# Four small edits to a two-block kernel: z's product in fp32r, a second swapped attention turn, one copy moved, and three wide products in the last pair

## The chip, the cores and the metric

The kernel runs on one core of a Trainium2 chip. The metric is device microseconds (us) of one execution. The engines are named as in the profile: PE (TensorE matmul), PEld (its weight load), DVE (VectorE), ACT (ScalarE), POOL (GpSimd) and SP (SyncE, which issues transfers). Line numbers such as L502 are those of the kernel before; in rows of the changed kernel the numbers are up to 14 higher.

## The reference

Two pre-LayerNorm blocks follow each other, on 2048 tokens of 512 channels, in fp32.

```python
h  = x + A(layernorm(x))        # linear attention, 32 heads of 16
h2 = h + B(layernorm(h))        # layernorm again, then an MLP over the tokens

# A
q, k, v = split(x @ wqkv)
phi = lambda a: concat(softmax(a @ w_phi), softmax(-(a @ w_phi)))   # per head
kv  = einsum("bhsf,bhsd->bhfd", phi(k), v)
z   = einsum("bhsf->bhf", phi(k))             # sum over all tokens
o   = (phi(q) @ kv) / ((phi(q) @ z) + 1e-6)
out = o @ wo

# B
u = gelu(einsum("bsd,sf->bdf", h, w1) + b1)   # 2048 -> 1792
y = einsum("bdf,fs->bds", u, w2) + b2         # 1792 -> 2048
```

## The kernel before

**Products.** An fp32 product is made of three fp32r products (fp32r: one pass of TensorE over fewer bits). `split` writes the high part of an operand by an ACT copy and the low part by a subtraction on DVE or POOL; `mm3` issues high·high (L69), high·low (L70) and low·high (L71). A few products are left in plain fp32, z's sum (L502) among them.

**Stages.** There are 16 tiles of 128 tokens (`NT`). First come the projections to q, k and v with the softmax exponentials, ordered by the scheduler and from the second last tile on written out by hand. Then z is made: the running sum `zacc` of the k exponentials gets its last tile by two DVE additions (L494) and is summed over the partitions by a product with a tile of ones (L502), which ACT copies to `zB` (L503). POOL multiplies `zB` into each tile's q exponentials (`s_ez`, L458).

**The attention loop** has 20 turns (`it`), and a turn works on several tiles at once. What a turn emits, engine by engine, is the order written in the loop: `s_pq` (POOL, L474), `s_ez` (POOL, L458), `s_den` (five DVE steps, ending in w), `s_tr` (PE transposes L548, copied by ACT to pht, L550), `s_num` (PE L567 reads pht; ACT copies the result to oh, L573), `s_ol` (DVE, L578), `s_wo` (PE, mm3 with oh and ol), `s_h` (residual, DVE L595), `s_moments` (ACT, L604 to L606, last of them ve), `s_rstd` (POOL, r, L611), `s_hn` (ACT L614, L624 and the high part L64, then POOL's subtraction L65 for the low part; both parts are called hs). `fills(it)` issues the first MLP product's work for an earlier tile, and reads hs: L69 needs only the high part, L70 the low one. In even turns `s_hn` stands ahead of `s_moments` and `s_tr`, in odd ones behind. Only at `it == TURN`, 6, does `s_ez` stand behind `s_hn`. At `it == TURN + 1` the additions for row sums of a tile (`q_sums`) are run once ahead of the rest.

**Sums for the MLP.** Later parts of the first MLP product are made by seven products of 2x2 blocks in place of eight, which need sums of blocks. `T_AT` is a table by turn and place in the turn that says when such sums (`t_sums`), their high parts (`t_hi`, "h0" to "h3", ACT L644, tile ht) and low parts (`t_lo`, "l0" to "l3", DVE L647) are issued.

**The second MLP product** has 8 pairs of token tiles, each of 7 steps (p) with seven block products. In `PROD` six products are wide: one 512-column matmul on the joined high and low part (L1111, whi) and one of 256 columns (L1111, wlo), each with a PSUM bank of its own; one is narrow, three matmuls of 256 columns (L1115). The last pair uses `LAST` with all seven narrow, two to a bank, four banks in all, and its results are put together on DVE (L1202 to L1219). Eight banks rotate.

**Ordering.** The attention loop and the second product have a manual order. Between the two, in the last columns of the first product (steps p = 6), PE is free to be ordered by the scheduler together with the first products of w2, and so are ACT and DVE.

Of the kernel before, what the change touches and what calls it, by code (L numbers as in the profile page):

```python
# [25 lines left out]
NG = 8  # L26
# [14 lines left out]
def block_kernel(ctx: ExitStack, tc: tile.TileContext, x, xT, wT, phic, wo, w1, b1, w2, b2,  # L41
                 kvmask, ident_in, out):
    nc = tc.nc
# [5 lines left out]
    ones = cst.tile([P, P], F32, name="ones")  # L49
# [4 lines left out]
    eps2 = cst.tile([P, 2], F32, name="eps2")  # L54
# [54 lines left out]
    X, XH, EQ, PK, VS, SQ, PS, W = {}, {}, {}, {}, {}, {}, {}, {}  # L109
# [68 lines left out]
    def turns(*lists):  # L178

        return [ops[i] for i in range(max(map(len, lists))) for ops in lists if i < len(ops)]  # L180

    def run(*lists):
        for op in turns(*lists):
            op()
# [5 lines left out]
        return e.rearrange("p g (a d) -> p (g a) d", d=DH)  # L190

    def k_ops(t, o):
        PK[t] = kk.tile([P, NG, P], F32, name="pk", bufs=len(V_NOT) + 5)
        run(logit_ops(o, PK[t], False))

    def k_logits(t):
# [10 lines left out]
    def k_norm(t, z=True):  # L207
        sk = wk.tile([P, 2 * H], F32, name="sk", bufs=2)
        nc.vector.reduce_sum(sk, heads(PK[t]), axis=AX.X)
        nc.vector.reciprocal(sk, sk)  # L210
        nc.gpsimd.tensor_mul(heads(PK[t]), heads(PK[t]), sk.unsqueeze(2).to_broadcast([P, 2 * H, DH]))  # L211
        if z and t == 0:
            nc.gpsimd.tensor_copy(zacc, PK[t])
        elif z:
            nc.gpsimd.tensor_add(zacc, zacc, PK[t])  # L215
# [158 lines left out]
    q = {"mm": 0, "logits": 0, "exp": 0, "sum": 0}  # L374
# [57 lines left out]

    ms = ExitStack()
    ms.enter_context(tc.manual_schedule(engines={ET.PE, ET.DVE, ET.Activation, ET.Pool}))
    k_norm(NT - 2, False)
    k_logits(NT - 1)
    ak1.close()
# [52 lines left out]
        wo_hi(j)  # L490
    v_kv()
    run(q_logits(0))
    for g in range(2):
        nc.vector.tensor_add(zacc[:, 4 * g:4 * g + 4, :], zacc[:, 4 * g:4 * g + 4, :], PK[NT - 1][:, 4 * g:4 * g + 4, :])  # L494
    for j in range(KD):
        wo_lo(j)
    negate()
    q_mm()
    zB = big.tile([P, NG, P], F32, name="zB", tag="big")
    for g in range(2):  # L500
        pz = ps_k.tile([P, 4, P], F32, name="pk_ps")
        nc.tensor.matmul(pz, ones, zacc[:, 4 * g:4 * g + 4, :], start=True, stop=True)  # L502
        nc.scalar.activation(zB[:, 4 * g:4 * g + 4, :], pz, AF.Identity, bias=eps2[:, 1:])  # L503
    q_exp(0)
    s_ez(0)
    s_ez(1)
# [27 lines left out]
    a2 = ExitStack()  # L534
# [164 lines left out]
    def fills(it):  # L699
        if FN[1] < it - LAG:  # L700
            fill(1, ps_q)
        if FN[0] <= it - LAG:
            fill(0, ps_f)

    T_AT = {(13, 2): "a0 b0", (14, 1): "c0 d0", (14, 2): "a2 b2", (14, 3): "h0", (15, 0): "h1", (15, 2): "c2 d2 l0", (15, 3): "h2",
            (16, 1): "l1", (16, 3): "l2", (17, 2): "a4 b4", (17, 3): "c4 d4 h3", (18, 2): "l3"}

    def t_at(it, place):
        for op in T_AT.get((it, place), "").split():
            i = int(op[1])  # L710
# [5 lines left out]
    for it in range(NT + 4):  # L716
        even = it % 2 == 0
        t_at(it, 0)
        if 0 <= it + 1 < NT:
            s_pq(it + 1)  # L720
        if it == 0:
            s_tr(0)
            s_kv()
        if it == 1:
            run(q_logits(0))
            q_mm()
            s_tr(1)
        if it > 1 and even and it <= NT:
            s_num(it // 2 - 1)
        t_at(it, 1)  # L730
        den = s_den(it + 2) if it + 2 < NT else []
        if it > 1 and even and it <= NT:
            ol = s_ol(it // 2 - 1)
            run(ol[:1] + den[:1] + ol[1:])
            den = den[1:]
        if it < NT:
            s_x(it)
        if it + 3 < NT and it != TURN:
            s_ez(it + 3)
        negate()  # L740
        q_mm()
        fills(it)
        q_exp(0)
        logits = q_logits(1)
        if it >= 4 and even:
            s_hn(it - 4)
        if it == TURN:
            s_ez(it + 3)
        if 3 <= it < NT + 3 and even:
            s_moments(it - 3)  # L750
        if it > 1 and even and it - 2 < NT:
            s_wo(it - 2)
        if 1 < it < NT:
            s_tr(it)
        if it > 1 and not even and it - 2 < NT:
            s_wo(it - 2)
        if it >= 4 and not even:
            s_hn(it - 4)
        if 3 <= it < NT + 3 and not even:
            s_moments(it - 3)  # L760
        if 3 <= it < NT + 3:
            s_rstd(it - 3)
        if it == TURN + 1:
            run(q_sums(0))
            flush()
        run(logits + (q_sums(0) if it > 0 else []), den)
        if it > 0:
            negate()
        if not logits:
            flush()  # L770
        t_at(it, 2)
        if 0 <= it - 2 < NT:
            s_h(it - 2)
        flush()
        t_at(it, 3)
# [149 lines left out]
    LAST = ((2, 1, 0, 0), (5, 5, 0, 1), (0, 0, 1, 0), (1, 4, 1, 1), (3, 6, 2, 0), (6, 2, 2, 1), (4, 3, 3, 0))  # L925
# [164 lines left out]
    for p in range(NEAR, NP):  # L1090
# [45 lines left out]
    for n, (sp, p) in enumerate(STEPS):  # L1136
        t = 2 * sp
        last = t + 2 == NT
# [4 lines left out]
                sums_w2()  # L1143
        if p == 0:
            bank = []
            for _ in range(4 if last else 7):
                pool = (ps_f, ps_q, ps_b, ps_b)[n_bank % 8 // 2]
                bank.append(pool.tile([P, 2, HD], F32, name="py", tag="pu"))
                n_bank += 1
        order = LAST if last else PROD  # L1150
        run_on = 3 if last else 2
        if p == 0:
            products(sp, [p], order[:-1] if n == 0 else order)
# [49 lines left out]
        hb = [uo.tile([P, 2, HD], F32, name=f"hb{i}", bufs=1) for i in range(2)]  # L1203
# [1 line left out]
            nc.sync.dma_start(flat(hb[i]), out[(t + i) * P:(t + i + 1) * P, :])  # L1205
            nc.vector.tensor_scalar(hb[i], hb[i], b2s[:, t + i:t + i + 1], None, op0=ALU.add)
        nc.scalar.activation(e[:, 1], bank[0][:, 0], AF.Copy)
        nc.vector.tensor_add(hb[1][:, 1], bank[0][:, 0], hb[1][:, 1])
        nc.vector.tensor_sub(u2, bank[0][:, 1], e[:, 1])
        nc.vector.tensor_sub(hb[1][:, 0], hb[1][:, 0], u2)  # L1210
        nc.vector.tensor_sub(u3, u2, bank[1][:, 0])
        nc.vector.tensor_add(hb[0], hb[0], u3.unsqueeze(1).to_broadcast([P, 2, HD]))
        nc.vector.tensor_add(hb[0][:, 0], bank[1][:, 1], hb[0][:, 0])
        nc.vector.tensor_sub(hb[1][:, 0], hb[1][:, 0], bank[1][:, 1])
        nc.vector.tensor_add(hb[0][:, 1], bank[2][:, 0], hb[0][:, 1])
        nc.sync.dma_start(out[t * P:(t + 1) * P, :], flat(hb[0]))
        for k, o, q in ((0, bank[2][:, 1], nc.scalar), (1, bank[3][:, 0], nc.sync)):
            nc.vector.tensor_add(hb[1][:, k], o, hb[1][:, k])
            q.dma_start(out[(t + 1) * P:NT * P, k * HD:(k + 1) * HD], hb[1][:, k])  # L1219

# [48 lines left out]
```

## Time and profile before

| | before |
|---|---|
| times | 516.42, 516.67, 516.90; median 516.67 us |
| profiled execution | 516.75 us, span 515.0 us |
| PE | 509.3 us busy, 99% of the span |
| DVE | 445.6 us, 87% |
| ACT | 297.7 us, 58% |
| POOL | 244.8 us, 48%, nearly all of it before 230 us |
| granted PE clock | full in all 40 slices of the span |

A row of the timeline reads: start in us, busy us, engine, line, operation, output <- input, sizes, how many instructions of the kind ran in succession, and in brackets the idle time ahead and who ended it. Starts count from the beginning of the span, which is about 1.75 us shorter than the execution's time.

### The profile page before, as it was taken

How to read it: one execution, taken by the hardware profiler on the slowest of the kernel's cores; microseconds unless marked ns; L12 is line 12 of the kernel's file. 1: busy time of each engine (PE TensorE's matmuls, PEld its weight loads, DVE VectorE, ACT ScalarE, POOL GpSimd, SP SyncE). 2: the span in 40 equal slices, each digit the busy share in tenths (PEclk: the TensorE clock that was granted, in tenths of full speed). 3: DMA queues.
4: the chain of work that ended last, by engine and by line, in shares of the span. 5: the costliest groups of instructions: out<-in, count | busy, mean ns of one | idle time of the engine just before them, and what ended most of it. 6: DMA issues, size and time to landing. Idle time of an engine off the chain costs nothing.

```text
span 515.0 us, 9359 instructions
## 1 busy us (share of the span) xinstructions
PE 509.3 (99%) x3546; PEld 438.9 (85%) x3546; DVE 445.6 (87%) x765; ACT 297.7 (58%) x494; POOL 244.8 (48%) x188
## 2 busy tenths in 40 slices
PE   8999999999999999999999999999999999999997
PEld 7888888887877777877788899998888898899897
DVE  6893999986689998877796998989989898998985
ACT  6998943424255886668976643457753444444430
POOL 2479799984999999975343300000002212211220
PEclk9999999999999999999999999999999999999999
DMA  8833311000041342334322233374136688668743
GB/s 309 278 125 120 85 48 32 1 1 2 11 156 41 103 140 86 124 124 122 113 92 83 82 105 103 102 245 140 45 123 127 159 185 166 138 148 191 165 52 74
DMA packets 36300, 58.56 MB, mean 114 GB/s; under 512 B 3744, under 2 KB 19360, under 8 KB 36256
## 3 DMA queue, kind: packets, MB, share of 16 engines
q1 hardware_dynamic: 31648, 50.85, 31.2%
q0 software_dynamic: 4032, 6.42, 9.3%
q8 instruction: 28, 0.46, 0.4%
q10 hardware_dynamic: 576, 0.69, 0.4%
q14 instruction: 16, 0.13, 0.1%
HBM read 46.81 MB, written 11.14 MB: 113 GB/s over the span
## 4 chain that ended last, share of the span: by engine, by line
PE 82%; POOL 11%; DVE 2%; ACT 2%; issue 1%; DMA 1%; SPq 0%; POOLq 0%
PE py L1111 20%; PE pu L941 12%; PE py L1115 7%; PE pu L69 7%; PE pu L70 6%; PE pu L71 6%; POOL ez L458 5%; POOL eq L474 3%; PE pv L70 3%; PE pk_ps L69 3%; PE pk_ps L70 2%; PE pk_ps L71 2%; PE pv L71 2%; PE pv L69 2%; POOL eq L176 2%; PE po L71 2%
## 5 line engine op out<-in xcount | busy, mean ns | idle before, releaser
L1187 POOL DMA_DIRECT2D out<-ot x7 | 6.2, 887 | 157.3 <-DMA wraw<-in_w 104.1
L997 ACT ACTIVATE whi<-wraw 128x1792 fp32r<-128x1792 f32 x28 | 47.7, 1703 | 44.2 <-DVE wraw L864 26.6
L1007 DVE TENSOR_TENSOR wlo<-wraw,whi 128x1792 fp32r<-128x1792 f32 x28 | 56.6, 2021 | 4.8 <-PE py L1115 4.6
L1111 PE MATMUL py<-uf,whi 128*128 128x512 f32 x210 | 57.6, 393 | 0.0
L70 PE MATMUL pu<-hs,whi 128*128 128x512 f32 x128 | 50.4, 394 | 0.2 <-POOL hs L65 0.2
L69 PE MATMUL pu<-hs,whi 128*128 128x512 f32 x128 | 50.1, 399 | 0.0
L71 PE MATMUL pu<-hs,wlo 128*128 128x512 f32 x128 | 47.9, 390 | 0.0
L458 POOL TENSOR_TENSOR ez<-eq,zB 128x1024 f32<-128x1024 f32 x16 | 38.8, 2428 | 4.5 <-ACT zB L503 4.5
L902 ACT ACTIVATE whi<-wraw 128x896 fp32r<-128x896 f32 x24 | 22.9, 955 | 31.1 <-PE pu L941 26.2
L1111 PEld LDWEIGHTS py<-uf,whi 128*128 128x128 f32 x210 | 35.8, 189 | 4.4
L1111 PEld LDWEIGHTS py<-uf,wlo 128*128 128x128 f32 x210 | 33.1, 190 | 4.6
L941 PE MATMUL pu<-ht,whi 128*128 128x256 f32 x192 | 35.6, 283 | 0.0
L1111 PE MATMUL py<-uf,wlo 128*128 128x256 f32 x210 | 34.9, 280 | 0.0
L211 POOL TENSOR_TENSOR pk<-pk,sk 128x1024 f32<-128x1024 f32 x16 | 31.1, 1944 | 6.6 <-DVE sk L210 6.6
L65 POOL TENSOR_TENSOR hs<-hb,hs 128x512 fp32r<-128x512 f32 x16 | 21.8, 1365 | 23.5 <-ACT hs L64 23.4
L550 ACT ACTIVATE pht<-tn 128x512 f32<-128x512 f32 x32 | 17.4, 597 | 26.8 <-PE tn L548 26.7
L474 POOL TENSOR_TENSOR eq<-eq,w 128x1024 f32<-128x1024 f32 x16 | 32.3, 2022 | 0.8 <-DVE w L471 0.8
L215 POOL TENSOR_TENSOR zacc<-zacc,pk 128x1024 f32<-128x1024 f32 x13 | 31.3, 2407 | 0.6
L69 PEld LDWEIGHTS pu<-hs,whi 128*128 128x128 f32 x128 | 24.0, 188 | 7.1 <-issue 2.5
L941 PEld LDWEIGHTS pu<-ht,whi 128*128 128x128 f32 x192 | 30.0, 192 | 0.0
L70 PEld LDWEIGHTS pu<-hs,whi 128*128 128x128 f32 x128 | 24.1, 188 | 5.8 <-POOL hs L65 1.4
L187 ACT ACTIVATE pk<-pk,r 128x1024 f32<-128x1024 f32 x16 | 18.4, 1150 | 18.3 <-DVE pk L165 18.3
(208 smaller groups left out, 1608.1 us busy)
## 6 DMA issues: line engine op xcount, KB each, us to landing
wraw<-in_w SPq DMA_DIRECT2D x28, 512.0 KB, 4.2
wraw<-in_w SPq DMA_DIRECT2D x48, 256.0 KB, 2.8
xraw<-in_xT SPq DMA_DIRECT2D x16, 256.0 KB, 3.2
xh<-in_x SPq DMA_DIRECT2D x16, 256.0 KB, 2.7
h<-in_x SPq DMA_DIRECT2D x16, 256.0 KB, 2.7
out<-h SPq DMA_DIRECT2D x14, 256.0 KB, 2.4
out<-ot POOLq DMA_DIRECT2D x14, 256.0 KB, 4.7
wraw<-in_wT SPq DMA_DIRECT2D x12, 256.0 KB, 5.0
```

Source lines behind the costliest of these rows:

```text
L69: nc.tensor.matmul(o, ah, bh, start=first, stop=False)
L70: nc.tensor.matmul(o, ah, bl, start=False, stop=False)
L71: nc.tensor.matmul(o, al, bh, start=False, stop=last)
L211: nc.gpsimd.tensor_mul(heads(PK[t]), heads(PK[t]), sk.unsqueeze(2).to_broadcast([P, 2 * H, DH]))
L215: nc.gpsimd.tensor_add(zacc, zacc, PK[t])
L458: nc.gpsimd.tensor_mul(EZ[t], EQ[t], zB)
L474: nc.gpsimd.tensor_mul(heads(EQ[t]), heads(EQ[t]), W[t].rearrange("p g c h -> p (g c h)").unsqueeze(2).to_broadcast([P, 2 * H, DH]))
L941: nc.tensor.matmul(ACC[p][bk][:, half], WS[p, i][x][:, a], hb[b][y], start=i == 0 and half == 0 and k == 0, stop=i == NT // 2 - 1 and k == ...
L997: nc.scalar.activation(WH[g], RAW[g], AF.Copy)
L1007: nc.vector.tensor_sub(wl_, RAW[g], WH[g])
L1111: nc.tensor.matmul(o, w, u, start=p == 0 and not low, stop=p == NP - 1, skip_group_check=True)
L1115: nc.tensor.matmul(bank[bk][:, half], AW[sp, p][x][:, a], UB[p, b][:, y], start=p == 0 and half == 0 and i == 0, stop=p == NP - 1 and i == ...
```

## The change

Four edits, independent of each other.

1. **z's product.** The sum `zacc` is split in a high part `zh` (ACT) and a low part `zl` (DVE), each half for itself, and the two fp32 products with ones become four fp32r ones, with a copy `ones_r` of the ones.
2. **The turn.** `TURN` becomes (6, 7). At it = 7 `s_hn(3)` now stands ahead of `s_moments` and `s_tr`, and `s_ez(10)` behind it. The additions of `q_sums`, of which turn 7 issued two sets, are issued once there.
3. **The table.** "h2", the high part of the third sum, moves from the end of turn 15 to the second place of turn 16.
4. **The last pair.** `ENDS` takes the place of `LAST` for the second product: products (2,1), (5,5) and (0,0) are wide, each with its own bank, so there are six banks, and three more DVE additions join the halves.

```diff
-TURN = 6
+TURN = (6, 7)
...
+    nc.scalar.activation(ones_r, ones, AF.Copy)
...
-    for g in range(2):
-        nc.vector.tensor_add(zacc[:, 4 * g:4 * g + 4, :], zacc[:, 4 * g:4 * g + 4, :], PK[NT - 1][:, 4 * g:4 * g + 4, :])
+    zh, zl = (kk.tile([P, NG, P], F32R, name=name, tag="pk", bufs=len(V_NOT) + 5) for name in ("zh", "zl"))
+    halves = [slice(4 * g, 4 * g + 4) for g in range(2)]
+    for a in halves:
+        nc.vector.tensor_add(zacc[:, a], zacc[:, a], PK[NT - 1][:, a])
+        nc.scalar.activation(zh[:, a], zacc[:, a], AF.Copy)
+    for a in halves:
+        nc.vector.tensor_sub(zl[:, a], zacc[:, a], zh[:, a])
...
-        nc.tensor.matmul(pz, ones, zacc[:, 4 * g:4 * g + 4, :], start=True, stop=True)
-        nc.scalar.activation(zB[:, 4 * g:4 * g + 4, :], pz, AF.Identity, bias=eps2[:, 1:])
+        nc.tensor.matmul(pz, ones_r, zh[:, a], start=True, stop=False)
+        nc.tensor.matmul(pz, ones_r, zl[:, a], start=False, stop=True)
+        nc.scalar.activation(zB[:, a], pz, AF.Identity, bias=eps2[:, 1:])
...
-    T_AT = {(13, 2): "a0 b0", (14, 1): "c0 d0", (14, 2): "a2 b2", (14, 3): "h0", (15, 0): "h1", (15, 2): "c2 d2 l0", (15, 3): "h2",
-            (16, 1): "l1", (16, 3): "l2", (17, 2): "a4 b4", (17, 3): "c4 d4 h3", (18, 2): "l3"}
+    T_AT = {(13, 2): "a0 b0", (14, 1): "c0 d0", (14, 2): "a2 b2", (14, 3): "h0", (15, 0): "h1", (15, 2): "c2 d2 l0",
+            (16, 1): "l1 h2", (16, 3): "l2", (17, 2): "a4 b4", (17, 3): "c4 d4 h3", (18, 2): "l3"}
...
-        if it + 3 < NT and it != TURN:
+        if it + 3 < NT and it not in TURN:
             s_ez(it + 3)
...
-        if it >= 4 and even:
+        if it >= 4 and (even or it in TURN):
             s_hn(it - 4)
-        if it == TURN:
+        if it in TURN:
             s_ez(it + 3)
...
-        if it >= 4 and not even:
+        if it >= 4 and not even and it not in TURN:
             s_hn(it - 4)
...
-        if it == TURN + 1:
-            run(q_sums(0))
+        adds = q_sums(0) if it > 0 else []
+        if it == TURN[1]:
+            run(adds)
             flush()
-        run(logits + (q_sums(0) if it > 0 else []), den)
+            adds = []
+        run(logits + adds, den)
...
+    ENDS = ((2, 1, 0, None), (5, 5, 1, None), (0, 0, 2, None), (1, 4, 3, 0), (3, 6, 3, 1), (6, 2, 4, 0), (4, 3, 5, 0))
...
-            for _ in range(4 if last else 7):
+            for _ in range(6 if last else 7):
...
-        order = LAST if last else PROD
+        order = ENDS if last else PROD
...
-        nc.vector.tensor_add(hb[1][:, 1], bank[0][:, 0], hb[1][:, 1])
-        nc.vector.tensor_sub(u2, bank[0][:, 1], e[:, 1])
+        nc.vector.tensor_add(e[:, 1], bank[0][:, 1], e[:, 1])
+        nc.vector.tensor_add(hb[1][:, 1], e[:, 1], hb[1][:, 1])
+        nc.vector.tensor_sub(u2, bank[1][:, 0], e[:, 1])
+        nc.vector.tensor_add(u2, bank[1][:, 1], u2)
         nc.vector.tensor_sub(hb[1][:, 0], hb[1][:, 0], u2)
-        nc.vector.tensor_sub(u3, u2, bank[1][:, 0])
+        nc.vector.tensor_sub(u3, u2, bank[2][:, 0])
+        nc.vector.tensor_sub(u3, u3, bank[2][:, 1])
```

POOL at turn 7, before: hs is the low part that `s_hn` makes, ez and eq belong to `s_ez` and `s_pq`, r to `s_rstd`.

```order
L611 TENSOR_TENSOR r_68<-ve_2185,mhalf 128x1
L474 TENSOR_TENSOR eq<-eq,w 128x1024
L458 TENSOR_TENSOR ez<-eq,zB 128x1024
L65 TENSOR_TENSOR hs<-hb,hs 128x512
L611 TENSOR_TENSOR r_68<-ve_2281,mhalf 128x1
```

The same place after the change:

```order
L619 TENSOR_TENSOR r_68<-ve_2195,mhalf 128x1
L476 TENSOR_TENSOR eq<-eq,w 128x1024
L65 TENSOR_TENSOR hs<-hb,hs 128x512
L460 TENSOR_TENSOR ez<-eq,zB 128x1024
L619 TENSOR_TENSOR r_68<-ve_2291,mhalf 128x1
```

hs has moved ahead of ez, one instruction earlier.

ACT in the same turn, before: L606 is the last step of `s_moments`, L550 the copies of the transposes (pht), L671 a weight's high part, L614, L624 and L64 the three steps of `s_hn(3)`.

```order
L606 ACTIVATE ve_2185<-ve_2185,eps_67 128x1
L550 ACTIVATE pht<-tn 128x4x128 x2
L671 ACTIVATE whi<-wraw 128x512 x2
L187 ACTIVATE eq<-eq,r_66 128x1024
L550 ACTIVATE pht<-tn 128x4x128 x2
L614 ACTIVATE ve_2185<-ve_2185,r_68 128x1
L624 ACTIVATE hb<-h,ve_2185,r_68 128x512
L64 ACTIVATE hs<-hb 128x512
```

After:

```order
L614 ACTIVATE ve_2195<-ve_2195,eps_67 128x1
L558 ACTIVATE pht<-tn 128x4x128 x2
L679 ACTIVATE whi<-wraw 128x512 x2
L188 ACTIVATE eq<-eq,r_66 128x1024
L622 ACTIVATE ve_2195<-ve_2195,r_68 128x1
L632 ACTIVATE hb<-h,ve_2195,r_68 128x512
L64 ACTIVATE hs<-hb 128x512
L558 ACTIVATE pht<-tn 128x4x128 x2
```

The three steps of `s_hn(3)`, which read POOL's r, have moved ahead of the second pair of pht copies.

ACT where turn 15 ends and turn 16 begins, before: ht is the copy that "h2" names, oh the copy of `s_num`.

```order
L606 ACTIVATE ve_2929<-ve_2929,eps_67 128x1
L644 ACTIVATE ht<-hb 128x1024
L671 ACTIVATE whi<-wraw 128x512
L573 ACTIVATE oh<-tn 128x512 x2
L614 ACTIVATE ve_2929<-ve_2929,r_68 128x1
```

After:

```order
L614 ACTIVATE ve_2939<-ve_2939,eps_67 128x1
L679 ACTIVATE whi<-wraw 128x512
L581 ACTIVATE oh<-tn 128x512 x2
L652 ACTIVATE ht<-hb 128x1024
L622 ACTIVATE ve_2939<-ve_2939,r_68 128x1
```

The copy ht has moved from ahead of whi and oh to behind them. On DVE z's two low parts (zl) come directly behind the two additions to zacc and ahead of wo's four low parts (wol). In the stretch between the first and the second MLP product, whose order the scheduler makes, instructions of PE, DVE and ACT are placed a few rows earlier or later; the order of SP's transfers is the same.

More of the change, by code (lines that the diff above doesn't have):

```diff
@@ L103, in block_kernel @@
     zacc = wp.tile([P, NG, P], F32, name="zacc")
+    ones_r = wp.tile([P, P], F32R, name="ones_r")
     ps_k = a1.enter_context(tc.tile_pool(name="ps_k", bufs=2, space=PSUM))
@@ L192, in k_ops @@
     def k_ops(t, o):
-        PK[t] = kk.tile([P, NG, P], F32, name="pk", bufs=len(V_NOT) + 5)
+        PK[t] = kk.tile([P, NG, P], F32, name="pk", tag="pk", bufs=len(V_NOT) + 5)
         run(logit_ops(o, PK[t], False))
@@ L499, in block_kernel @@
     zB = big.tile([P, NG, P], F32, name="zB", tag="big")
-    for g in range(2):
+    for a in halves:
         pz = ps_k.tile([P, 4, P], F32, name="pk_ps")
-        nc.tensor.matmul(pz, ones, zacc[:, 4 * g:4 * g + 4, :], start=True, stop=True)
-        nc.scalar.activation(zB[:, 4 * g:4 * g + 4, :], pz, AF.Identity, bias=eps2[:, 1:])
+        nc.tensor.matmul(pz, ones_r, zh[:, a], start=True, stop=False)
+        nc.tensor.matmul(pz, ones_r, zl[:, a], start=False, stop=True)
+        nc.scalar.activation(zB[:, a], pz, AF.Identity, bias=eps2[:, 1:])
     q_exp(0)
@@ L1207, in block_kernel @@
         nc.scalar.activation(e[:, 1], bank[0][:, 0], AF.Copy)
-        nc.vector.tensor_add(hb[1][:, 1], bank[0][:, 0], hb[1][:, 1])
-        nc.vector.tensor_sub(u2, bank[0][:, 1], e[:, 1])
+        nc.vector.tensor_add(e[:, 1], bank[0][:, 1], e[:, 1])
+        nc.vector.tensor_add(hb[1][:, 1], e[:, 1], hb[1][:, 1])
+        nc.vector.tensor_sub(u2, bank[1][:, 0], e[:, 1])
+        nc.vector.tensor_add(u2, bank[1][:, 1], u2)
         nc.vector.tensor_sub(hb[1][:, 0], hb[1][:, 0], u2)
-        nc.vector.tensor_sub(u3, u2, bank[1][:, 0])
+        nc.vector.tensor_sub(u3, u2, bank[2][:, 0])
+        nc.vector.tensor_sub(u3, u3, bank[2][:, 1])
         nc.vector.tensor_add(hb[0], hb[0], u3.unsqueeze(1).to_broadcast([P, 2, HD]))
-        nc.vector.tensor_add(hb[0][:, 0], bank[1][:, 1], hb[0][:, 0])
-        nc.vector.tensor_sub(hb[1][:, 0], hb[1][:, 0], bank[1][:, 1])
-        nc.vector.tensor_add(hb[0][:, 1], bank[2][:, 0], hb[0][:, 1])
+        nc.vector.tensor_add(hb[0][:, 0], bank[3][:, 0], hb[0][:, 0])
+        nc.vector.tensor_sub(hb[1][:, 0], hb[1][:, 0], bank[3][:, 0])
+        nc.vector.tensor_add(hb[0][:, 1], bank[3][:, 1], hb[0][:, 1])
         nc.sync.dma_start(out[t * P:(t + 1) * P, :], flat(hb[0]))
-        for k, o, q in ((0, bank[2][:, 1], nc.scalar), (1, bank[3][:, 0], nc.sync)):
+        for k, o, q in ((0, bank[4][:, 0], nc.scalar), (1, bank[5][:, 0], nc.sync)):
             nc.vector.tensor_add(hb[1][:, k], o, hb[1][:, k])
```

## The prediction

> **What bounds the kernel now.** I read the head of the page first, then the waits of TensorE, then the windows of the two stretches in which the change moves instructions, and last the timeline at each of the edited places.
>
> ```profile
> span 515.0 us, 9359 instructions
> ...
> PE 509.3 (99%) x3546; PEld 438.9 (85%) x3546; DVE 445.6 (87%) x765; ACT 297.7 (58%) x494; POOL 244.8 (48%) x188
> ```
>
> TensorE is busy 509.3 of 515.0 us. A change gains only by taking matmul time out of PE's row, or by ending one of its few waits; time on any other engine counts only where PE stands for it. Two such waits are listed that belong to edited steps:
>
> ```profile
> PE po L71 <- DVE ol L578: 0.2, 1, 0.2
> ...
> PE pu L70 <- POOL hs L65: 0.2, 1, 0.2
> ```
>
> Each is one event of 0.2 us. The timeline shows more than the list does, since a matmul that waits is partly drawn as a longer one; I measure a stall as the distance between the starts of neighbouring matmuls less their usual distance. How close the other engines follow is in the windows (columns: PE, PEld, DVE, ACT, POOL busy, then PE clock, DMA share, GB/s):
>
> ```profile
> 165.00:206.00 41.00, 40.84 (x282) 31.70 (x266) 38.87 (x68) 32.02 (x66) 40.66 (x29) 1.00 0.34 110
> ...
> 290.00:355.00 65.00, 65.00 (x525) 64.20 (x525) 59.47 (x130) 32.49 (x41) 0.00 (x0) 1.00 0.45 134
> ```
>
> In the attention loop around turns 4 to 8 (165 to 206 us) POOL is busy 40.66 of 41.00 us beside PE's 40.84: the two run in lock-step, and an earlier PE finds POOL late unless POOL moves up too. From 290 to 355 POOL is out, and DVE with 59.47 of 65 is nearest. The clock is 1.00 in all of these rows.
>
> The profiled execution took 516.75 us, 0.08 above the median of 516.67; what lies outside its span, 1.75 us, I leave as it is. A measurement of this kernel tells 0.2% (1.03 us) from no change, so "faster" begins below 515.64 and "slower" above 517.70.
>
> **Edit 1, z in fp32r.** First the rows of z and of what feeds and uses it:
>
> ```profile
> 122.45 2.15 DVE L494 TENSOR_TENSOR zacc<-zacc,pk 128x512 f32<-128x512 f32 x2
> 124.53 2.48 DVE L446 TENSOR_TENSOR wol<-wor,woh 128x512 fp32r<-128x512 f32 x4
> ...
> 125.90 1.88 PE L502 MATMUL pk_ps<-zacc,ones 128*128 128x512 f32 x4
> ...
> 127.85 0.39 PE L70 MATMUL pv<-wvl,xs 128*128 128x512 f32 x1
> ...
> 128.58 4.77 POOL L458 TENSOR_TENSOR ez<-eq,zB 128x1024 f32<-128x1024 f32 x2 [4.52 <-ACT zB L503]
> ...
> 164.59 0.55 POOL L611 TENSOR_TENSOR r<-ve,mhalf 128x1 f32<-128x1 f32 x1 [0.95 <-ACT ve L606]
> ```
>
> The usual distance of 512-column fp32r matmuls is 0.23 us: six of them start at 486.62 and the next kind at 488.00 (rows under edit 4), 1.38 / 6. From 125.90 to 127.85 is 1.95 and holds z's product and one such matmul (L69), so the product costs 1.95 − 0.23 = 1.72 for its four records. After it, four fp32r matmuls cost 4 × 0.23 = 0.92. PE saves **0.80**. The Trainium skill's page "FP8 and Floating Point Precision", section "TensorE Precision Notes", says that a true fp32 product takes four passes through the array. By it the two products would be eight passes of 0.23, 1.84, and the gain 0.92; the trace shows four records over 1.72, which is near it, and the row decides.
>
> The new operands must not be late. DVE's two adds end at 122.45 + 2.15 = 124.60. ACT's copy of the second half costs 0.63 (row at 191.15 below, the same form) and ends at 125.25, DVE's two subtractions cost 2.48 / 4 = 0.62 each and end at about 125.95. PE wants the last of them as its fourth matmul, at 125.90 + 0.69 = 126.59. That is 0.64 in hand. The four wol subtractions behind them are pushed by 1.24 to about 128.3; they are first read two turns into the loop, far behind. zB is then out 0.6 to 0.8 earlier, POOL's first ez with it: POOL had stood 4.52 us for exactly this. So POOL moves up with PE, and where it waits later (0.95 at 164.59 for ACT's ve, which itself follows PE) the releaser is early too. The 0.80 therefore goes through the lock-step stretch. Bounds: 0.3 if zl comes 0.5 late, 0.92 at most; I take 0.80.
>
> **Edit 2, the turn at it = 7.** Its rows:
>
> ```profile
> 188.05 0.99 POOL L611 TENSOR_TENSOR r<-ve,mhalf 128x1 f32<-128x1 f32 x1
> ...
> 191.00 2.38 POOL L458 TENSOR_TENSOR ez<-eq,zB 128x1024 f32<-128x1024 f32 x1
> 193.35 1.29 POOL L65 TENSOR_TENSOR hs<-hb,hs 128x512 fp32r<-128x512 f32 x1
> ...
> 199.36 1.75 POOL L65 TENSOR_TENSOR hs<-hb,hs 128x512 fp32r<-128x512 f32 x1
> ```
>
> ```profile
> 189.00 1.09 ACT L550 ACTIVATE pht<-tn 128x512 f32<-128x512 f32 x2 [0.44 <-PE tn L548]
> 189.97 0.30 ACT L614 ACTIVATE ve<-ve,r 128x1 f32<-128x1 f32 x1
> 190.30 0.82 ACT L624 ACTIVATE hb<-h,ve,r 128x512 f32<-128x512 f32 x1
> 191.15 0.63 ACT L64 ACTIVATE hs<-hb 128x512 fp32r<-128x512 f32 x1
> ```
>
> ```profile
> 191.63 1.09 PE L567 MATMUL tn<-pht,kvB 64*32 64x256 f32 x32
> ...
> 194.14 0.39 PE L69 MATMUL pu<-hs,whi 128*128 128x512 f32 x1
> 194.69 0.50 PE L70 MATMUL pu<-hs,whi 128*128 128x512 f32 x1 [0.16 <-POOL hs L65]
> 195.03 0.40 PE L71 MATMUL pu<-hs,wlo 128*128 128x512 f32 x1
> ```
>
> The low part of tile 3 (hs, POOL) came at 194.64. PE's L70 started 194.69 − 194.14 = 0.55 behind L69, 0.32 over the usual, and the next 0.34 behind that, 0.11 over: a stall of 0.43. With hs ahead of ez (2.38) on POOL it is ready two us sooner and the stall goes. Two things take most of it back. First, ACT now does tile 3's three steps before the pht copies. They wait for POOL's r, which ends at 189.04, by edit 1 at 188.24. Then 0.30 + 0.82 + 0.63 with the small gaps of the rows brings 190.0, and the two copies end at 191.1. PE's L567 reads them; it starts at 191.63 now, and at 190.83 by edit 1. It would stand about 0.3. Second, the next hs (tile 4) ended at 201.11, and PE's L70 stood 0.11 for it; since POOL is full, it moves up by edit 1's 0.80 and no more, so whatever PE won beyond that at tile 3 is waited out there. Net I take **0.1** (0.43 − 0.3, rounded down for the second). Bounds: +0.54 when neither bites (0.43 and 0.11), −0.4 when the copies come 0.5 later than I reckon. That the additions for tile 7's row sums are made once in place of twice changes nothing on PE.
>
> **Edit 3, the h2 copy.** Its rows:
>
> ```profile
> 249.21 1.05 ACT L644 ACTIVATE ht<-hb 128x1024 fp32r<-128x1024 f32 x1
> 250.16 0.61 ACT L671 ACTIVATE whi<-wraw 128x512 fp32r<-128x512 f32 x1
> 250.68 1.07 ACT L573 ACTIVATE oh<-tn 128x512 fp32r<-128x512 f32 x2
> ```
>
> ```profile
> 251.78 1.29 DVE L578 TENSOR_TENSOR ol<-tn,oh 128x512 fp32r<-128x512 f32 x2 [1.31 <-ACT oh L573]
> ```
>
> ```profile
> 251.97 0.39 PE L70 MATMUL po<-wol,oh 128*128 128x512 f32 x1
> 252.52 0.50 PE L71 MATMUL po<-woh,ol 128*128 128x512 f32 x1 [0.17 <-DVE ol L578]
> 252.86 0.39 PE L69 MATMUL po<-woh,oh 128*128 128x512 f32 x1
> ```
>
> PE stands (0.55 − 0.23) + (0.34 − 0.23) = 0.43 for ol, which DVE makes from ACT's oh; DVE itself stands 1.31 for oh. The 128x1024 copy of 1.05 us stood ahead on ACT and now comes behind, so oh is up to 0.95 earlier and ol likewise: covered twice over. The copy itself is wanted by a later subtraction (l2, a turn on). Gain **0.43**; bounds 0 (another ACT row holds oh) and 0.43.
>
> **Edit 4, the last pair.** Its rows, from the timeline, the chain that ended last, and the tail:
>
> ```profile
> 486.62 1.55 PE L1111 MATMUL py<-uf,whi 128*128 128x512 f32 x6
> 488.00 0.88 PE L1111 MATMUL py<-uf,wlo 128*128 128x256 f32 x6
> 488.71 0.40 PE L1115 MATMUL py<-uf,whi 128*128 128x256 f32 x2
> ```
>
> ```profile
> 494.13 17.64 PE py L1115 x147
> ```
>
> ```profile
> 511.79 0.42 DVE L1218 TENSOR_TENSOR hb<-py,hb 128x256 f32<-128x256 f32 x1 [0.32 <-PE py L1115]
> ```
>
> 147 narrow matmuls in 17.64 us are 0.120 each, 0.360 for the three of a product. A wide one (1.38 / 6 = 0.230) with its 256-column partner (0.71 / 6 = 0.118) is 0.348. Three products over 7 steps change, 21 × 0.012 = **0.25**. The end hangs on DVE's last adds, which wait for PE's last product (0.32) and stay as they are; the three added adds (0.42 each) belong to the banks of the first two products, which are finished earlier, so I set them at nothing. If one of them does not fit, the end is up to 0.4 later. Bounds −0.15 and 0.25.
>
> **Sum.** 0.80 + 0.10 + 0.43 + 0.25 = 1.58. From the profiled 516.75 that is 515.17; from the median, 516.67 − 1.58 = 515.09, forecast **515.1**.
>
> **The rivals.** (B) The turn gives all of its 0.54: 516.67 − 2.02 = 514.65. For it: POOL's hs at 199.36 took 1.75 where the one at 193.35 took 1.29, as a DVE subtraction had started just before it:
>
> ```profile
> 199.21 0.74 DVE L665 TENSOR_TENSOR wlo<-wraw,whi 128x512 fp32r<-128x512 f32 x1
> ```
>
> Were their order turned, POOL would have 0.46 more. On this the Trainium skill's page "SBUF — State Buffer", section "SBUF: two separate sides", has a rule: the port pair that DVE and GpSimd share is an exclusive lock, held for a whole instruction by the one that starts first. The trace agrees with it here (0.46 longer behind a start 0.15 earlier); which of them starts first after the change is open. Against it: ACT's new wait for POOL's r lies on PE's path however the port goes. Chance 0.13.
>
> (C) The turn loses instead: ACT's copies come 0.5 later than reckoned, and PE and the later tiles follow. Gain 1.58 − 0.5 = 1.08, 515.6, on the bound of 515.64. Chance 0.16, half of it on either side.
>
> (D) The lead is taken back by DVE between 290 and 355. Its lead on PE is small in places:
>
> ```profile
> 352.25 0.69 DVE L665 TENSOR_TENSOR wlo<-wlo,whi 128x512 fp32r<-128x512 f32 x1 [0.52 <-issue]
> ```
>
> ```profile
> 353.28 0.61 PE L71 MATMUL pu<-hs,wlo 128*128 128x512 f32 x2
> ```
>
> Here the low part is ready 353.28 − 352.94 = 0.34 before PE reads it. An early PE loses what exceeds this: 1.33 of lead (edits 1 to 3) less 0.34 is 1.0, so the time would be 516.67 − 0.34 − 0.25 = 516.1, no change. Against it: DVE has 5.5 us idle in those 65, so most of its work moves up with PE. Chance 0.08.
>
> (E) Slower. The stretch from 352 to 380 (the eight steps of w1's last columns, mixed with the first products of w2) is ordered by a scheduler, and the change reorders PE, ACT and DVE in it.
>
> ```profile
> 352.00:380.00 28.00, 28.00 (x134) 23.46 (x133) 26.11 (x52) 18.30 (x32) 0.00 (x0) 1.00 0.33 104
> ```
>
> PE has no gap there now, but DVE is busy 26.11 of 28. If one more DVE instruction of the 0.69 kind falls ahead of a wlo with 0.34 in hand, PE stands 0.35; over the eight steps 2.8, or 516.67 − 1.58 + 2.8 = 517.9. A late 128x1792 copy ahead of one of them would make it more. It decides the sign from a total of 1.58 on, and "slower" from 2.6. Against it: the new order puts wlo no later among its neighbours as far as the rows can be told apart. Chance 0.11.
>
> That z's product gains nothing because four matmuls take as long as two fp32 ones is excluded by the 0.23 rows: fp32r costs one record each.
>
> **The numbers.** Forecast 0.52, B 0.13, C 0.16, D 0.08, E 0.11. Faster: 0.52 + 0.13 + 0.08 = 0.73; within 0.2%: 0.08 + 0.08 = 0.16; slower 0.11. The range from 514.3 (B with an early zl and 0.92) to 516.3 (D, with 0.2 for the spread of runs) leaves out E and the ends.
>
> **What would show it.** In the profile after: z's four matmuls 0.23 apart and POOL's first ez near 127.8; at tile 3 no step between L69 and L70, but L567 waiting for ACT's pht; ol's wait near 252 gone; the last pair 0.25 shorter; no new PE wait between 345 and 385. The forecast is wrong if PE's new waits on POOL at tile 4 or on wlo after 345 sum to over 0.6, or if a zl matmul waits.

## The result and the profile after

The changed kernel takes 515.05 us (median of 8 runs, 514.78 to 515.77) against 516.61 for the kernel before (8 runs, 516.15 to 517.08): 1.56 us less, ratio 0.9971 with the interval 0.9962 to 0.998, that is 1.0 to 2.0 us (here and below the ratio is worked out over all runs, so it can differ a little from the quotient of the medians). The forecast was 515.1. The profiled execution's span went from 515.0 to 513.3.

The head of the page after, and PE's waits after (us in total, times, longest):

```profile
span 513.3 us, 9324 instructions
...
PE 508.0 (99%) x3525; PEld 437.8 (85%) x3525; DVE 447.7 (87%) x770; ACT 298.8 (58%) x497; POOL 245.2 (48%) x188
```

```profile
PE tn L575 <- ACT pht L558: 0.2, 1, 0.2
```

PE is busy 1.3 us less. The waits for ol and for hs are off the list, and a wait for ACT's pht is new. Now the edited places in the timeline after, z first:

```profile
124.31 1.33 DVE L501 TENSOR_TENSOR zl<-zacc,zh 128x512 fp32r<-128x512 f32 x2
125.55 2.49 DVE L448 TENSOR_TENSOR wol<-wor,woh 128x512 fp32r<-128x512 f32 x4
...
125.52 0.39 PE L509 MATMUL pk_ps<-zh,ones_r 128*128 128x512 f32 x1
125.75 0.39 PE L510 MATMUL pk_ps<-zl,ones_r 128*128 128x512 f32 x1
125.98 0.39 PE L509 MATMUL pk_ps<-zh,ones_r 128*128 128x512 f32 x1
126.20 0.39 PE L510 MATMUL pk_ps<-zl,ones_r 128*128 128x512 f32 x1
...
126.66 0.39 PE L70 MATMUL pv<-wvl,xs 128*128 128x512 f32 x1
...
127.52 5.14 POOL L460 TENSOR_TENSOR ez<-eq,zB 128x1024 f32<-128x1024 f32 x2 [3.83 <-ACT zB L511]
```

The four matmuls are 0.23 apart and none waits for zl. From the first of them to L70 it is 126.66 − 125.52 = 1.14 where it was 1.95: 0.81 saved. But POOL's first two ez now take 5.14 where they took 4.77: the last of the four wol is on DVE from about 127.4 to 128.04, and ez starts at 127.52. Seven us on, PE stands for it:

```profile
130.34 1.22 DVE L469 TENSOR_REDUCE tz<-ez 128x64 f32<-128x1024 f32 x1 [2.29 <-POOL ez L460]
...
133.83 0.68 DVE L162 TENSOR_TENSOR eq<-pu,mx 128x512 f32<-128x512 f32 x1
...
134.36 0.39 PE L71 MATMUL pv<-wvh,xs 128*128 128x512 f32 x1
134.65 0.47 PE L69 MATMUL pu<-wqh,xs 128*128 128x512 f32 x1
134.96 0.39 PE L70 MATMUL pu<-wql,xs 128*128 128x512 f32 x1
```

L69 opens a new product of q, whose place in PSUM DVE clears with L162 (end 134.51); it starts 0.29 behind L71 and L70 0.31 behind it, 0.14 lost together. DVE's steps before L162 start with tz, which stood 2.29 for POOL's first ez.

The turn, ACT, POOL and PE:

```profile
188.07 0.29 ACT L622 ACTIVATE ve<-ve,r 128x1 f32<-128x1 f32 x1 [0.53 <-POOL r L619]
188.39 0.82 ACT L632 ACTIVATE hb<-h,ve,r 128x512 f32<-128x512 f32 x1
189.24 0.64 ACT L64 ACTIVATE hs<-hb 128x512 fp32r<-128x512 f32 x1
189.78 1.06 ACT L558 ACTIVATE pht<-tn 128x512 f32<-128x512 f32 x2
...
189.99 1.28 POOL L65 TENSOR_TENSOR hs<-hb,hs 128x512 fp32r<-128x512 f32 x1
...
198.34 1.76 POOL L65 TENSOR_TENSOR hs<-hb,hs 128x512 fp32r<-128x512 f32 x1
...
190.90 1.10 PE L575 MATMUL tn<-pht,kvB 64*32 64x256 f32 x32 [0.21 <-ACT pht L558]
...
193.42 0.39 PE L69 MATMUL pu<-hs,whi 128*128 128x512 f32 x1
193.65 0.39 PE L70 MATMUL pu<-hs,whi 128*128 128x512 f32 x1
...
199.76 0.39 PE L69 MATMUL pu<-hs,whi 128*128 128x512 f32 x1
200.16 0.50 PE L70 MATMUL pu<-hs,whi 128*128 128x512 f32 x1
```

Tile 3's low part is there at 191.3, over two us ahead of its use, and L69 to L70 is the usual 0.23. ACT had to stand 0.53 for POOL's r first, so the pht copies end at 190.84 and PE's L575 starts 0.60 behind its predecessor (190.30) where it was 0.32: 0.28 lost. At tile 4 POOL's subtraction takes 1.76 again and L70 is 0.40 behind L69.

The h2 place, and the last pair (the chain's last row, one pair's step in the timeline, and DVE's last addition):

```profile
248.78 1.06 ACT L581 ACTIVATE oh<-tn 128x512 fp32r<-128x512 f32 x2
...
249.87 1.29 DVE L586 TENSOR_TENSOR ol<-tn,oh 128x512 fp32r<-128x512 f32 x2 [0.35 <-ACT oh L581]
...
251.02 0.39 PE L70 MATMUL po<-wol,oh 128*128 128x512 f32 x1
251.25 0.39 PE L71 MATMUL po<-woh,ol 128*128 128x512 f32 x1
```

```profile
505.81 4.33 PE py L1126 x36
```

```profile
500.01 0.86 PE L1122 MATMUL py<-uf,whi 128*128 128x512 f32 x3
500.71 0.52 PE L1122 MATMUL py<-uf,wlo 128*128 128x256 f32 x3
501.06 0.40 PE L1126 MATMUL py<-uf,whi 128*128 128x256 f32 x2
...
510.16 0.42 DVE L1232 TENSOR_TENSOR hb<-py,hb 128x256 f32<-128x256 f32 x1 [0.65 <-PE py L1126]
```

oh and ol are early enough, and PE goes from L70 to L71 at the usual 0.23. Three wide products take 501.06 − 500.01 = 1.05, 0.350 each, a narrow one 4.33 / 12 = 0.361. The last addition still waits for PE alone, so the three new ones cost nothing at the end. In the stretch that the scheduler orders, and in the one before it, PE has no gap:

```profile
290.00:355.00 65.00, 65.00 (x525) 64.22 (x524) 59.57 (x131) 33.43 (x44) 0.00 (x0) 1.00 0.46 138
352.00:380.00 28.00, 28.00 (x134) 23.43 (x133) 26.58 (x51) 19.48 (x32) 0.00 (x0) 1.00 0.32 101
```

**Where the 1.7 us of the span come from.** The start of one and the same matmul in two timelines gives PE's lead at that place. This table has it for every kernel of the study, against the profile of before (starts there in brackets; "pht" are the products L567 near those times).

| kernel | z's product (125.90) | behind z (127.85) | po of kvS (141.45) | pht (177.47) | pht (191.63) | pht (206.13) | first ht (292.00) | last (511.47) |
|---|---|---|---|---|---|---|---|---|
| changed kernel | 0.37 | 1.19 | 1.02 | 1.04 | 0.73 | 0.95 | 1.40 | 1.63 |
| z alone | 0.50 | 1.32 | 1.18 | 1.14 | 1.17 | 1.17 | 1.18 | 1.18 |
| turn alone | 0.57 | 0.56 | 0.57 | 0.55 | 0.27 | 0.54 | 0.55 | 0.55 |
| h2 alone | -0.06 | -0.06 | -0.06 | -0.06 | -0.05 | -0.07 | 0.38 | 0.38 |
| last pair alone | 0.21 | 0.21 | 0.21 | 0.21 | 0.18 | 0.15 | 0.12 | 0.35 |
| all but the turn | -0.21 | 0.61 | 0.45 | 0.44 | 0.41 | 0.39 | 0.85 | 1.07 |
| repeat of changed | -0.02 | 0.80 | 0.63 | 0.63 | 0.34 | 0.59 | 1.05 | 1.28 |
| repeat of all but the turn | 0.23 | 1.05 | 0.90 | 0.91 | 0.91 | 0.91 | 1.37 | 1.60 |
| four wol later | 0.01 | 0.83 | -4.74 | -6.51 | -6.79 | -6.51 | -6.05 | -5.82 |
| r behind eq | 0.16 | 0.98 | 0.82 | 0.75 | -0.30 | 0.29 | 0.75 | 0.97 |
| the same, no turn | -0.22 | 0.60 | 0.44 | 0.37 | -0.69 | -1.42 | -0.96 | -0.73 |
| r behind eq, one wol first | 0.33 | 1.14 | 1.15 | 1.06 | 0.03 | 0.61 | 1.07 | 1.30 |
| one wol first | 0.60 | 1.42 | 1.42 | 1.39 | 1.11 | 1.37 | 1.82 | 2.04 |

The first column is no edit's: it runs from -0.22 to 0.60, and "turn alone", whose program up to there is that of before, has 0.57. It arises in the first 9 us and then stays. There PE's 128-column matmuls start 0.21 apart at first and 0.11 apart later; the spacing changes at 4.0 us in the changed kernel (lead 0.37) and at 7.0 us in "all but the turn" (lead -0.21). The profile of before changes at 4.2 us, but then stands 0.35 for DVE's wraw, whose load came late (DVE had stood 1.07 for it). The columns behind the first are read as differences along a row. Where a row holds no edit it still drifts by up to 0.09 ("last pair alone" goes from 0.21 to 0.12 ahead of its edit), so a difference under 0.1 is not told from nothing.

### The profile page after: what moved, and what is told of

The parts are those of the page before. It is cut to its first block, busy times and chain, and to the rows that moved or that the text cites. A ratio compares the mean times of both kernels' runs of the same rounds, so it can differ in the third digit from the quotient of the medians.

```text
span 513.3 us, 9324 instructions
## 1 busy us (share of the span) xinstructions
PE 508.0 (99%) x3525; PEld 437.8 (85%) x3525; DVE 447.7 (87%) x770; ACT 298.8 (58%) x497; POOL 245.2 (48%) x188
## 4 chain that ended last, share of the span: by engine, by line
PE 86%; POOL 9%; DVE 1%; issue 1%; ACT 1%; DMA 1%; POOLq 0%
PE py L1122 21%; PE pu L951 12%; PE pu L69 7%; PE pu L70 7%; PE pu L71 7%; PE py L1126 5%; POOL ez L460 4%; PE pv L70 3%; PE pv L71 3%; PE pv L69 3%; PE pk_ps L69 3%; PE pk_ps L71 2%; PE pk_ps L70 2%; POOL eq L476 2%; PE po L71 2%; PE po L69 2%
## 5 line engine op out<-in xcount | busy, mean ns | idle before, releaser
L1122 PE MATMUL py<-uf,whi 128*128 128x512 f32 x225 | 61.9, 393 | 0.0
L70 PE MATMUL pu<-hs,whi 128*128 128x512 f32 x128 | 50.3, 393 | 0.0
L69 PE MATMUL pu<-hs,whi 128*128 128x512 f32 x128 | 50.1, 399 | 0.0
L71 PE MATMUL pu<-hs,wlo 128*128 128x512 f32 x128 | 48.0, 390 | 0.0
L1122 PEld LDWEIGHTS py<-uf,whi 128*128 128x128 f32 x225 | 38.4, 189 | 4.6
L1122 PEld LDWEIGHTS py<-uf,wlo 128*128 128x128 f32 x225 | 35.5, 190 | 5.0
L1122 PE MATMUL py<-uf,wlo 128*128 128x256 f32 x225 | 37.5, 280 | 0.0
L69 PEld LDWEIGHTS pu<-hs,whi 128*128 128x128 f32 x128 | 24.0, 188 | 7.1 <-issue 2.5
L70 PEld LDWEIGHTS pu<-hs,whi 128*128 128x128 f32 x128 | 24.1, 188 | 5.5 <-POOL hs L65 1.0
```

Source lines behind the costliest of these rows:

```text
L69: nc.tensor.matmul(o, ah, bh, start=first, stop=False)
L70: nc.tensor.matmul(o, ah, bl, start=False, stop=False)
L71: nc.tensor.matmul(o, al, bh, start=False, stop=last)
L1122: nc.tensor.matmul(o, w, u, start=p == 0 and not low, stop=p == NP - 1, skip_group_check=True)
```

## The experiments: each edit alone

The first four runs make one edit each, as in the diff above, and nothing else.

> Edit 1 alone (z's product in fp32r, the rest as before). Theory (terms of the prediction add up, the part of the lead that was there ahead of z is chance of the first loads): z's four matmuls 0.23 apart, PE 0.8 earlier behind them, about 0.15 of that lost again at the first q product behind 134 us (PE waits for a PSUM bank that DVE frees, DVE being held by POOL's ez); time 0.6 to 0.8 below before. Rival (the lead ahead of z belongs to the edit): PE is 0.35 earlier already at the start of z, time 1.1 to 1.2 below. Rival (POOL caps it): the lead is used up between 165 and 206 us, time 0 to 0.3 below.

515.96 us against 516.57, ratio 0.9988 (0.998 to 0.9997). PE's lead grows by 0.82 at z, falls by 0.14 up to the po product, and stays. That is 0.68 for the edit, the theory's number. The rival by which the 0.35 ahead of z belong to the edit falls with the first column: this run has 0.50 there, but "turn alone", without edit 1, has 0.57, and two later runs with edit 1 have -0.02 and -0.21. The cap between 165 and 206 us falls too: 1.14 at 177.47 and 1.17 at 206.13.

> Edit 2 alone (turn (6, 7)). Theory: the stall of 0.43 at tile 3's low part goes, PE stands 0.3 at the product that reads ACT's pht copies and some at tile 4's low part; net within 0.15 of nothing, time 0 to 0.15 below before, not told from it. Rival (the turn gives its full 0.54): 0.5 below. Rival (it loses): 0.3 above.

516.53 against 516.57, ratio 1.0003 (0.9994 to 1.0012). The timeline of PE has both halves of the exchange:

```profile
190.75 0.39 PE L71 MATMUL po<-woh,ol 128*128 128x512 f32 x1
191.36 1.10 PE L567 MATMUL tn<-pht,kvB 64*32 64x256 f32 x32 [0.22 <-ACT pht L550]
...
200.26 0.39 PE L69 MATMUL pu<-hs,whi 128*128 128x512 f32 x1
200.62 0.50 PE L70 MATMUL pu<-hs,whi 128*128 128x512 f32 x1
```

0.28 is lost at L567 (0.61 for 0.32), and 0.13 at tile 4 before L70 (0.36 for 0.23). In the table the lead is 0.55 before and 0.54 behind. Edit 2 gives nothing here; with edit 1 the run without the turn, below, shows the same.

> Edit 3 alone (h2 moved behind oh). Theory: PE's stall of 0.43 at the low part ol near 252 us goes and nothing takes its place; time 0.4 below before. Rival: the copy's new place delays what stands behind it on ACT (tile 12's three steps, the next pht) and PE stands there; time 0 to 0.2 below.

516.34 against 516.57, ratio 0.9992 (0.9983 to 1.0001). The lead goes from -0.07 to 0.38: 0.45, as the theory said; the time alone could not tell it from nothing.

> Edit 4 alone (three wide products in the last pair). Theory: the last pair's matmuls take 0.25 less, the tail is as long as before; time 0.25 below. Rival: the three additional additions push the last ones, the end is 0.4 later behind the last matmul, time 0.15 above.

516.38 against 516.57, ratio 0.9998 (0.9989 to 1.0007). The lead goes from 0.12 to 0.35: 0.23. The rival's 0.4 at the end did not come.

> The changed kernel without edit 2 (turn 6 alone). Theory (edit 2 moves the wait and removes none): tile 3's low part stalls PE 0.43 again, the wait for pht is gone, behind tile 4's low part PE is where it was with edit 2; time within 0.15 of the changed kernel, 1.3 to 1.6 below before. Rival (edit 2 gives 0.43 once edit 1 has moved POOL): 0.4 above the changed kernel.

515.51 us against 516.47, ratio 0.9977 (0.9968 to 0.9986). Between 177.47 and 206.13 the lead falls by 0.05, in the changed kernel by 0.09. That is the theory's nothing. The median by itself, 0.46 above the changed kernel's, would have looked like the rival; but this kernel was 0.58 behind the changed one already at the start of z, and a repeat (below) gave 514.98.

## The experiments: what holds the rest

**Four wol later.** The edit:

```diff
-    for j in range(KD):
-        wo_lo(j)
     negate()
...
     run(s_den(1))
     run(q_logits(0))
+    for j in range(KD):
+        wo_lo(j)
```

> The changed kernel with wo's four low parts on DVE moved from behind zl to behind the second tile's den and row logits. Theory (POOL's first ez is held up by DVE's wol, which the two zl push into it; DVE's q chain follows ez and frees PE's bank late): the first ez takes 2.4 in place of 2.78, PE's wait of 0.14 at the q product near 134.7 goes; what POOL has won is gone at its wait for ve at 163.6, so the time is 0.14 below the changed kernel and no more. Rival (POOL's lead lasts through the loop): 0.4 to 0.5 below, with the waits at tiles 0, 1 and 4 gone.

522.21 us against 516.47, ratio 1.0114 (1.01 to 1.0127), 5.7 slower. The timeline has the reason of the wait and of what followed it (last row: the window from 140 to 150 us, PE clock in the third column from the end):

```profile
127.88 4.76 POOL L460 TENSOR_TENSOR ez<-eq,zB 128x1024 f32<-128x1024 f32 x2 [3.84 <-ACT zB L509]
...
138.49 7.31 DVE L448 TENSOR_TENSOR wol<-wor,woh 128x512 fp32r<-128x512 f32 x4
```

```profile
146.19 0.69 PE L564 MATMUL po<-ident,kvS 128*128 128x128 f32 x2 [5.41 <-DVE kvS L530]
...
147.10 0.63 PE L70 MATMUL pu<-wql,xs 128*128 128x512 f32 x1
147.52 0.63 PE L71 MATMUL pu<-wqh,xs 128*128 128x512 f32 x1
...
140.00:150.00 10.00, 4.59 (x19) 3.64 (x17) 9.88 (x13) 2.50 (x4) 5.17 (x4) 0.66 0.66 212
```

The first half of the theory holds: the two ez take 4.76, and the lead at the q product is no longer lost there. The place for the four was wrong. In a stretch in which POOL runs one SBUF product behind the other they took 7.31 us where they take 2.49 (the first two 2.44 and 2.83, each ending 0.55 behind the end of a POOL product, eq and then ez), kvS behind them on DVE came late, and PE stood 5.41. Neither theory had this.

**r behind eq.** POOL had stood 0.94 us for ACT's ve at 163.56 in the changed kernel. The first form of this experiment put the call of `s_rstd(0)` behind the `run` of the row logits:

> The changed kernel with POOL's r of tile 0 (turn 3) moved behind the two steps of the row logits, so that POOL does these while it had stood 0.94 us for ACT's ve. Theory (POOL caps PE from 165 to 206 us): POOL is 0.9 earlier for the rest of the stretch, PE's stalls at the low parts of tiles 0, 1 and 4 (0.11, 0.25, 0.2) and at pht in turn 7 (0.28) go; time 0.6 to 0.8 below the changed kernel. Rival (PE's stalls are ACT's or DVE's, POOL is only named): 0 to 0.2 below.

> The same move of r, without edit 2. Theory: with POOL 0.9 earlier tile 3's low part comes in time without edit 2, and no pht waits for POOL; time as in the run with r moved and edit 2 kept, or up to 0.2 lower. Rival (tile 3's low part still comes late): 0.3 above that run.

Both left every engine's order as it was, since POOL's two steps are issued by `negate()`, one line further down. So these are repeats, of the changed kernel (515.21 against 516.47, ratio 0.9975, 0.9966 to 0.9984) and of it without the turn (514.98, ratio 0.9972, 0.9961 to 0.9982), and they say how far such a median moves between two series of runs. The second form moves the instruction:

```diff
-        if 3 <= it < NT + 3:
+        if 3 < it < NT + 3:
             s_rstd(it - 3)
...
         if it > 0:
             negate()
+        if it == 3:
+            s_rstd(0)
```

> The changed kernel with POOL's r of tile 0 really behind the two row-logit steps of turn 3 (in the run before it had stayed ahead of them, since these are issued by the call that follows). Theory (POOL's lateness from 165 to 206 us comes from its wait of 0.94 us for ACT's ve): POOL fills that wait, the steps behind start 0.9 earlier, PE's stalls at the low parts of tiles 0, 1 and 4 (0.11, 0.16, 0.2) and at pht in turn 7 (0.28) go, 0.7 in all; time 0.6 to 0.75 below the changed kernel. Rival (r later holds up ACT's three steps of tile 0, and POOL stands again for its next operands): 0 to 0.3 below.

515.84 us against 516.42, ratio 0.9986 (0.9977 to 0.9995), some 0.7 to 1.0 behind the changed kernel's gain. POOL does what was meant: r at 164.12 without a wait, the next eq at 164.64 in place of 165.43. The stalls that the theory names are gone too. But the gain does not come. The same DVE subtraction in the changed kernel, and then with r moved:

```profile
164.49 1.53 DVE L673 TENSOR_TENSOR wlo<-wraw,whi 128x512 fp32r<-128x512 f32 x1
```

```profile
164.12 0.55 POOL L619 TENSOR_TENSOR r<-ve,mhalf 128x1 f32<-128x1 f32 x1
164.64 1.94 POOL L476 TENSOR_TENSOR eq<-eq,w 128x1024 f32<-128x1024 f32 x1
...
164.69 2.44 DVE L673 TENSOR_TENSOR wlo<-wraw,whi 128x512 fp32r<-128x512 f32 x1
...
186.65 0.39 PE L70 MATMUL pu<-hs,whi 128*128 128x512 f32 x1
187.16 0.50 PE L71 MATMUL pu<-hs,wlo 128*128 128x512 f32 x1
```

POOL's eq now starts 0.05 ahead of DVE's wlo, which waits it out and takes 2.44. Two more of them go from 1.16 and 0.80 to 2.04 and 1.46. DVE is late, PE stands for it at 178, 181 and 187 (there 0.28 before L71, which reads wlo), and the lead falls by 1.05 between 177.47 and 191.63. Of that 0.59 comes back by 206.13, as the stalls that before has at tiles 3 and 4 are not met. From z's start to the last matmul this kernel wins 0.81, the changed one 1.26: POOL's early steps took more from DVE than they gave.

> The same without edit 2. Theory: POOL's 0.9 also covers the 0.43 at tile 3, so edit 2 is not needed: time within 0.1 of the run with edit 2, no stall over 0.1 left between 165 and 206 us. Rival: tile 3's stall stays in part, 0.2 to 0.4 above that run.

516.99 us against 516.42, ratio 1.0006 (0.9997 to 1.0015), 1.15 behind the run with the turn. Here two wlo take 4.02 us, h behind them is late, and PE stands for it:

```profile
189.14 4.02 DVE L673 TENSOR_TENSOR wlo<-wraw,whi 128x512 fp32r<-128x512 f32 x2
...
195.96 0.39 PE L71 MATMUL pu<-hs,wlo 128*128 128x512 f32 x1
197.33 0.47 PE L69 MATMUL po<-woh,oh 128*128 128x512 f32 x1 [0.98 <-DVE h L603]
```

Neither theory was right: tile 3's low part is in time, but the order of POOL's steps decides which DVE subtractions are held.

**One wol first.** Of the four, one moves into DVE's wait of 1.16 us ahead of the last row logits before z; first together with r behind eq, then alone.

```diff
     v_kv()
+    wo_lo(0)
     run(q_logits(0))
...
-    for j in range(KD):
+    for j in range(1, KD):
         wo_lo(j)
```

> r behind the row logits, and besides one of wo's four low parts moved ahead on DVE, into its wait of 1.16 us before the last row logits ahead of z. Theory (the fourth wol overlaps the start of POOL's first ez and costs it 0.37 us): the two ez take 4.77 in place of 5.14, PE's wait of 0.14 near 134.7 us goes; the lead behind it is 0.1 to 0.15 more than in the run without this move. Rival (the moved wol holds up POOL's last pk and with it zacc and zl): PE stands at zl, 0.1 to 0.5 later.

515.43 us against 516.42, ratio 0.9983 (0.9974 to 0.9992). The two ez take 4.76, and the lead behind z stays: 1.14 and 1.15, where the run without this move had 0.98 and 0.82. Behind 177 us it loses as that run does.

> The changed kernel with only the one low part of wo moved ahead on DVE, r where the changed kernel has it. Theory (what the last runs left standing): the two first ez take 4.76 in place of 5.14, PE's wait of 0.14 near 134.7 us goes and POOL follows PE behind its wait for ve, so the lead of 0.13 lasts to the end; time 0.1 to 0.15 below the changed kernel, less than the runs can tell apart, and seen only in the starts of PE's matmuls. Rival (the phases of DVE and POOL between 165 and 206 us shift against each other, as when r was moved): 0.2 to 0.5 above the changed kernel.

```profile
118.81 0.63 DVE L448 TENSOR_TENSOR wol<-wor,woh 128x512 fp32r<-128x512 f32 x1
119.06 2.17 POOL L212 TENSOR_TENSOR pk<-pk,sk 128x1024 f32<-128x1024 f32 x1 [1.10 <-DVE sk L211]
...
127.30 4.76 POOL L460 TENSOR_TENSOR ez<-eq,zB 128x1024 f32<-128x1024 f32 x2 [3.83 <-ACT zB L512]
```

514.94 us against 516.64, ratio 0.9968 (0.9956 to 0.998). The wol delays POOL's pk by 0.2, which nobody waits for, and the 0.82 of z is kept whole (1.42 behind z and at po). From z's start to the last matmul this kernel wins 1.44, the changed one 1.26 and its repeat 1.30. By this measure it is the best of the study, and the gain over the changed kernel is 0.14 to 0.18; the times alone do not tell the two apart.

## Why the prediction was right, and where it was not

By the lead along the rows the edits give 0.82 − 0.17 − 0.07 + 0.45 + 0.23 = 1.26 us (z, its loss at the q product, the turn, h2, last pair). The forecast's sum was 1.58. The medians gave 1.56 and, in the repeat, 1.26, both inside the intervals of each other. So sign, range and cause were right. That the point was met within 0.05 us is luck: the other 0.3 of the 1.56 belongs to no edit, and it happens to fill what the four terms came short of the forecast.

- **Edit 1, 0.80 forecast, 0.65 to 0.68 found.** The price of the product was right (0.82). The step that failed is "the four wol subtractions behind them are pushed by 1.24 … far behind": I asked only who reads wol, and not whom it meets. It met POOL's first ez (5.14 for 4.77); with one of the four wol moved and the rest equal, the first ez takes 2.40 in place of 2.78, which shows that this is the cause, since both the 0.37 and PE's loss go with the one wol moved.
- **Edit 2, 0.10 forecast, -0.09 to -0.01 found.** The mechanism came as written: 0.43 gone, 0.28 at pht (forecast 0.3), the rest at tile 4. The term that was mis-sized is the second, tile 4, for which 0.43 − 0.3 was only rounded down by 0.03: L70 stands 0.13 to 0.17 there, all that was left. What is found is no more than the drift of a row, so it is told as nothing and not as a loss. One reading was wrong and costs nothing: the additions for row sums are as many as before (16 sets on DVE in both), and the second of turn 7's two sets is made a turn later.
- **Edit 3, 0.43 forecast, 0.45 found; edit 4, 0.25 forecast, 0.23 found.** Both as costed. DVE's wait for oh fell from 1.31 to 0.35 us, and the added additions fit.
- **The rivals.** B needed POOL to start hs ahead of DVE's wlo at tile 4; wlo started 0.08 earlier, and hs took 1.76 as before. C's extra 0.5 did not come. Nor did D and E: from 292 us to the last matmul the lead goes from 1.40 to 1.63, the 0.23 of the last pair, and nothing is lost on the way.
- **"The two run in lock-step" was half of it.** That POOL moves up with PE was right: edit 1's lead lasts from 165 to 206 us. But moving POOL alone up by 0.8 made the kernel slower, as DVE's two-input subtractions then ran into it. In this stretch the two runs with r moved show PE bounded by POOL and DVE together, by the order in which they meet and not by POOL's sum of busy time.

## What to carry to other kernels

When work is pushed on one engine, look at what it now overlaps on the neighbour that shares its access to SBUF, not only at who reads its result. A wait of 0.4 us that a swap removes is worth what the next two waits on the same path leave of it, so count them before claiming it. Gains of half a per mille are read from the lead of the same instruction in two profiles, section by section, since the first 9 us alone move a run by up to 0.8 us.

## What the runs showed of the hardware

- DVE subtractions with both inputs in SBUF (128x512, 0.62 us each in a row of four) took 1.8 us each on average when POOL ran SBUF products without a break (7.31 for four: 2.44, 2.83, 0.73 and 1.54); POOL's 128x1024 ones grew from 2.4 to 2.8 when a DVE subtraction had just started. The Trainium skill, page "SBUF — State Buffer", section "SBUF: two separate sides", calls the port pair they share an exclusive lock for a whole instruction; these numbers agree. They add that in a row it is not every instruction of DVE that waits: two of the four waited out a POOL product, and the third went through at once.
- After PE had stood 5.41 us, its 512-column matmuls started 0.43 apart for some 3 us (147.10 to 147.52, usual 0.23), with a granted clock of 0.66 over those 10 us; the wait cost 7.3 us in all (lead 0.83 behind z, -6.51 at 177.47). The granted clock fell to 0.50 at 143.0, 2.3 us after PE's last matmul, and was full again at 149.9, 3.7 us after PE had started again. The Trainium skill, page "TensorE: Matmul & The Clock Gate", section "Part 1: The HAM clock gate (the "warmup" mystery)", has the clock halved after an idle window of about 3.4 us, and back after as long a busy one. The way back agrees with it; the way down came sooner than that figure, and no run here shows why. None of the shorter waits in the other runs, up to 0.98 us once the first 10 us are over, had such a tail: their granted clock is 1.00 from there to the last matmul.
